# Every second FFN1 chunk of the first block in a bank of attention's pool

## The chip, the cores and the metric

The kernel runs on one core of a Trainium2 chip. The metric is the device time of one execution in microseconds. The core has a matrix engine (PE), a vector engine (DVE), a scalar engine (ACT), a general engine (POOL) and a queue that issues the transfers (SP). Each engine takes its instructions in the order in which they stand in its queue, and waits at the head of the queue until what that instruction needs is there. Matmul results land in eight accumulation banks of 128 x 512 fp32 each.

## The reference

Eight batches of 576 rows go through linear attention with a norm per head, and then through a mixing layer and a two-layer FFN with a residual:

```python
kv = np.einsum('bhsd,bhse->bhde', k, v)
out = np.einsum('bhsd,bhde->bhse', q, kv)
out = out / rms(out) * g_norm                  # rms over the 64 columns of a head
x = out.transpose(0, 2, 1, 3).reshape(B, S, H * D)        # 8 x 576 x 512
u = x + (x.transpose(0, 2, 1) @ U @ V).transpose(0, 2, 1)
y = u + np.maximum(u @ w_ch1, 0.0) @ w_ch2     # 512 -> 2048 -> 512
```

The weights come in as 64-bit floats; the kernel decodes their bits to fp32 itself.

## The kernel before

Attention runs batch by batch and, in a batch, over four pairs of heads. The FFN runs over nine blocks of 512 rows (`j` 0 to 8). A block goes through the 2048 hidden columns in 16 chunks `f` of 128. For a chunk,

- F1(f) (`ffn1`, lines 365 to 367) is 12 matmuls of 128 x 512 into one bank: four slices of the inner dimension, each as three products, because every operand is split into a high and a low part;
- `relu` evicts that bank in two steps: hh(f) on ACT (line 374), the rounded result, and hl(f) on DVE (line 375), what the rounding left over. hl(f) is the last reader of the bank. hh and hl have two buffers each (`hp`);
- F2(f) (`ffn2`, line 382) is 12 matmuls that add to the four output banks `y`: four with hh and the high weights, four with hl, four with hh and the low weights. They run in order of f.

While block 0 runs, the weights of its later chunks are still being decoded: for each 128 x 512 weight tile ACT takes an absolute value (line 80), DVE does four operations (lines 83, 84, 86, 88), ACT rounds the result (line 93), POOL takes the rest (line 94). The loop over the chunks asks for the decode of w1(f+3) and w2(f+3) ahead of chunk f. Beside that the attention of batch 1 is laid into block 0 (`STEPS0`): for each pair p a step kv(p) (lines 194, 198; ACT copies the result with line 101), out(p) (lines 217, 219, and much DVE work up to line 272), t(p) (lines 287, 289; read by lines 301 and 302) and mix(p) (line 357, read by line 359). Each takes one or two banks of the pool `ps_p`, whose tiles are called `pp`. After block 0 the same goes on with batch 2 in block 1, and so on, with no more weights to decode.

The eight banks are four for the outputs `y` (pool `ps_y`), one for FFN1 (`ps_h`, tile `h`), three for attention (`ps_p`, tile `pp`). FFN1 of chunk 0 of block 0 has a `pp` bank already (`hs`, line 485), since it starts ahead of the loop. A new tile of a pool takes a bank that an earlier tile of it has left, and so waits for the last reader of that earlier tile.

The text of the kernel isn't the order on the engines. When the program is built, a scheduler puts the instructions of each engine in an order, by its own estimate of when their operands are there; it also picks which of the three `pp` banks a tile gets. That order is fixed when the kernel runs.

Of the kernel before, what the change touches and what calls it, by code (L numbers as in the profile page):

```python
# [10 lines left out]
F32 = mybir.dt.float32  # L11
# [9 lines left out]
P = 128  # L21
# [8 lines left out]
BLK = 512  # L30
# [17 lines left out]
def build(ctx: ExitStack, tc: tile.TileContext, kv_in, kvt0_in, kvt_in, q_in, uv_in, g_in, w1, w2, out):  # L48
# [10 lines left out]
    ps_h = ctx.enter_context(tc.tile_pool(name="ps_h", bufs=1, space=bass.MemoryType.PSUM))  # L59
    ps_p = ctx.enter_context(tc.tile_pool(name="ps_p", bufs=3, space=bass.MemoryType.PSUM))  # L60
# [91 lines left out]
    def decode_w(which, f, tmp=None, n=None):  # L152
        if tmp is None:
            tmp = st.tile([P, DM], F32, name="st")
        decode(raws.pop((which, f)), tmp, n)
        w = weight_slot(f"{which}s{f}", [P, 2, DM], F32R, which, f)
        if n is None:
            split(w[:, 0], w[:, 1], tmp, nc.gpsimd)
        else:
            move("wh", n, w[:, 0], tmp)  # L160
            minus("wl", n, w[:, 1], tmp, w[:, 0].bitcast(F32))
        w_sb[which][f] = [w[:, s].rearrange("p (d c) -> p d c", c=P) for s in range(2)]
# [199 lines left out]
    def ffn1(h, f, ds, j):  # L362
        uh, ul = ut[j]
        for d in ds:
            nc.tensor.matmul(h, lhsT=w1s[f][0][:, d, :], rhs=uh[:, d, :], start=(d == 0), stop=False)  # L365
            nc.tensor.matmul(h, lhsT=w1s[f][0][:, d, :], rhs=ul[:, d, :], start=False, stop=False)  # L366
            nc.tensor.matmul(h, lhsT=w1s[f][1][:, d, :], rhs=uh[:, d, :], start=False, stop=(d == ND - 1))  # L367

    def relu(h, end=False):
        if end:  # L370
            hh, hl = [sc.tile([P, BLK], F32R, name=f"h{s}_end", tag=f"x{s}") for s in "hl"]
        else:
            hh, hl = [hp.tile([P, BLK], F32R, name=f"h{s}") for s in "hl"]
        nc.scalar.activation(out=hh, in_=h, func=AF.Relu)  # L374
        nc.vector.scalar_tensor_tensor(out=hl, in0=h, scalar=0.0, in1=hh.bitcast(F32), op0=ALU.max, op1=ALU.subtract)  # L375
        return hh, hl

    def ffn2(y, hs):
        for c, cols, acc in y:
            for f, hh, hl in hs:  # L380
                for w, h in ((0, hh), (0, hl), (1, hh)):
                    nc.tensor.matmul(acc, lhsT=w2s[f][w][:, c, :], rhs=h[:, cols], start=(f == 0 and w == 0 and h is hh),  # L382
                                     stop=(f == NF - 1 and w == 1))

    def finish(y, j):
        uh, ul = ut.pop(j)
        for c, cols, acc in y:
            if j == NBLK - 1:
                o = ut32[c][:, S - BLK + cols.start:S - BLK + cols.stop]
                nc.vector.scalar_tensor_tensor(out=o, in0=o, scalar=g_sb, in1=acc, op0=ALU.mult, op1=ALU.add)  # L390
            else:
                o = st.tile([P, DM], F32, name="st")
                nc.vector.tensor_tensor(out=o, in0=acc, in1=uh[:, c, :].bitcast(F32), op=ALU.add)  # L393
                nc.gpsimd.tensor_tensor(out=o, in0=o, in1=ul[:, c, :].bitcast(F32), op=ALU.add)  # L394
            nc.sync.dma_start(out=out[j, c][:, cols], in_=o)

    def outputs(j):

        y = [(c, slice(0, BLK), ps_y.tile([P, BLK], F32, name="y")) for c in range(ND)]
        if j == NBLK - 1:  # L400
            c, _, acc = y.pop()
            y.append((c, slice(0, BLK // 2), acc[:, 0:BLK // 2]))
            y.append((c, slice(BLK // 2, BLK), ps_p.tile([P, BLK], F32, name="pp")[:, 0:BLK // 2]))
        return y
# [85 lines left out]
    def prep_schedule(b):  # L490

        todo = {}
        if 0 < b <= B:
            todo[1] = [lambda: [split_cols(b - 1, c, 1, nc.gpsimd) for c in range(ND)]]
        if b < B:
            for p in range(NPAIR):
                steps = STEPS0 if b == 1 else STEPS
                base = steps["gap"] * p

                def kv(p=p):  # L500
                    kv_step(b, p)
                    nxt = (b, p + 1) if p + 1 < NPAIR else (b + 1, 0)
                    if nxt[0] < B:
                        load_kv(*nxt)

                def o(p=p):
                    for what in (out_step, stats_step, mul_step, xsplit_step, turn_step):
                        what(b, p)
                    nxt = (b, p + 1) if p + 1 < NPAIR else (b + 1, 0)
                    if nxt[0] < B:  # L510
                        load_q(*nxt)

                def t(p=p):
                    t_step(b, p)
                    t4_step(b, p)

                for at, what in (("kv", kv), ("out", o), ("t", t), ("mix", lambda p=p: mix_step(b, p))):
                    todo.setdefault(base + steps[at], []).append(what)
        return todo
# [3 lines left out]
    for j in range(NBLK):  # L523
        todo = prep_schedule(j + 1)
        y = None
        for f in range(NF):
            if j == 0:
                for which in ("w1", "w2"):
                    while ahead[which] < min(NF, f + 1 + AHEAD[which]):
                        decode_w(which, ahead[which])  # L530
                        ahead[which] += 1
            end = False
            if j == 0 and f < NEARLY:
                h = hs[f]
                ffn1(h, f, [3], j)
            else:
                end = j == NBLK - 1 and f == NF - 1
                h = ps_p.tile([P, BLK], F32, name="pp") if end else ps_h.tile([P, BLK], F32, name="h")
                ffn1(h, f, range(ND), j)
            hcur = (f, *relu(h, end))  # L540
            for w in todo.get(2 * f, []):
                w()
            if hprev is not None and not (j == NBLK - 1 and f > NF - 3):
                ffn2(y_prev if f == 0 else y, [hprev])
            if f == 0:
                if j > 0:
                    finish(y_prev, j - 1)
                y = outputs(j)
            for w in todo.get(2 * f + 1, []):
                w()  # L550
            held = (held + [hcur])[-3:]
            hprev = hcur
        y_prev = y
# [59 lines left out]
```

## Time and profile before

| | us |
|---|---|
| median of 3 runs | 943.87 (943.43 to 944.83) |
| the profiled execution | 944.59 |
| its span on the core | 942.8 |
| PE busy in the span | 913.3 (4570 matmul records) |
| DVE busy | 446.0 |
| ACT busy | 255.8 |
| POOL busy | 141.8 |

The profiled execution is 1.8 us longer than its span, for what lies around the first and the last instruction. A matmul record lasts about 0.39 us, but matmuls are pipelined: one starts about 0.23 us after the other when nothing is in the way, and that pitch is what counts. A busy engine of nearly 100% means a queue that never waits; the idle time of an engine is named with what ended it.

In the rows, `h<-uth,w1s` is FFN1, `y<-hh,w2s` and `y<-hl,w2s` are FFN2, `hh<-h` and `hl<-h` the two steps of `relu`, `st<-w1raw,st` and the like the decode of a weight tile. `PE` is the matmul itself, `PEld` the load of its stationary operand.

### The profile page before, as it was taken

The numbers are of one execution on the slowest core, as the hardware profiler recorded it, in microseconds if no ns is written. First come the engines' busy times: TensorE is split into PE (matmuls) and PEld (weight loads), VectorE is DVE, ScalarE is ACT, GpSimd is POOL, SyncE is SP. The second block draws the span as 40 slices with busy tenths as digits, with TensorE's granted clock in tenths as the row PEclk, the third lists the DMA queues.
The fourth block names the chain that finished last, engine by engine and source line by source line (L and its number), as shares of the span: only waits on it lengthen the run. The fifth ranks groups of instructions, "written<-read, shape, count | busy, mean of one in ns | idle before, by whom it ended". The sixth has DMA issues, their size and how long they took to land.

```text
span 942.8 us, 12401 instructions
## 1 busy us (share of the span) xinstructions
PE 913.3 (97%) x4570; PEld 762.8 (81%) x4570; DVE 446.0 (47%) x941; ACT 255.8 (27%) x565; POOL 141.8 (15%) x134
## 2 busy tenths in 40 slices
PE   7879889999999999999999999999999999999998
PEld 7757667888888888888888888888888888888887
DVE  6999997644354435443454344443543331112112
ACT  5534554322222222222232223222322221111110
POOL 4454442200020002000020002000200020002000
PEclk9999999999999999999999999999999999999999
DMA  9951121322121113121222112211211010001001
GB/s 351 407 206 31 36 62 36 122 57 66 42 96 56 54 26 109 44 78 26 74 71 82 27 54 93 73 34 44 91 53 26 13 45 1 1 0 46 1 1 45
DMA packets 45037, 65.50 MB, mean 69 GB/s; under 512 B 9904, under 2 KB 28080, under 8 KB 44976
## 3 DMA queue, kind: packets, MB, share of 16 engines
q1 hardware_dynamic: 44976, 64.71, 20.8%
q8 instruction: 36, 0.59, 0.3%
q14 instruction: 25, 0.20, 0.1%
HBM read 46.97 MB, written 9.44 MB: 60 GB/s over the span
## 4 chain that ended last, share of the span: by engine, by line
PE 85%; DVE 11%; issue 1%; SPq 1%; DMA 1%; ACT 0%; DVEq 0%; ACTq 0%
PE y L382 38%; PE h L365 13%; PE h L366 13%; PE h L367 13%; PE pp L217 2%; PE pp L194 2%; DVE st L86 2%; DVE st L88 1%; DVE st L83 1%; SPq L275 1%; DVE st L84 1%; PE pp L287 1%; PE pp L357 1%; DVE hl L375 1%; PE pp L289 1%
## 5 line engine op out<-in xcount | busy, mean ns | idle before, releaser
L382 PE MATMUL y<-hh,w2s 128*128 128x512 f32 x1144 | 374.7, 395 | 4.6 <-ACT hh L374 3.9
L375 DVE SCALAR_TENSOR_TENSOR hl<-h,hh 128x512 fp32r<-128x512 f32 x142 | 97.6, 688 | 334.2 <-ACT hh L374 334.1
L382 PEld LDWEIGHTS y<-hh,w2s 128*128 128x128 f32 x1144 | 208.4, 189 | 45.8 <-ACT hh L374 5.8
L365 PE MATMUL h<-uth,w1s 128*128 128x512 f32 x568 | 224.6, 395 | 12.6 <-DVE hl L375 12.6
L366 PE MATMUL h<-utl,w1s 128*128 128x512 f32 x568 | 222.9, 393 | 0.0
L382 PE MATMUL y<-hl,w2s 128*128 128x512 f32 (+1 forms) x572 | 222.5, 390 | 0.0
L367 PE MATMUL h<-uth,w1s 128*128 128x512 f32 x568 | 222.3, 391 | 0.0
L374 ACT ACTIVATE hh<-h 128x512 fp32r<-128x512 f32 x142 | 84.8, 597 | 394.4 <-PE h L367 394.2
L365 PEld LDWEIGHTS h<-uth,w1s 128*128 128x128 f32 x568 | 107.3, 189 | 39.3 <-DVE hl L375 14.3
L367 PEld LDWEIGHTS h<-uth,w1s 128*128 128x128 f32 x568 | 107.4, 189 | 23.3
L382 PEld LDWEIGHTS y<-hl,w2s 128*128 128x128 f32 x572 | 108.1, 189 | 21.9
L366 PEld LDWEIGHTS h<-utl,w1s 128*128 128x128 f32 x568 | 107.3, 189 | 21.6
L113 POOL TENSOR_TENSOR xl<-x,xh 128x512 fp32r<-128x512 f32 x32 | 43.2, 1349 | 492.2 <-ACT xh L101 488.3
L394 POOL TENSOR_TENSOR st<-st,utl 128x512 f32<-128x512 f32 x32 | 41.0, 1303 | 154.0 <-DVE st L393 153.7
L359 DVE TENSOR_TENSOR ut<-pp,ut 128x288 f32<-128x288 f32 x56 | 24.7, 456 | 34.0 <-DMA ut<-xt 18.6
L322 ACT ACTIVATE uth<-ut,g_sb 128x448 fp32r<-128x448 f32 (+7 forms) x56 | 27.7, 531 | 43.9 <-DVE ut L359 39.7
L393 DVE TENSOR_TENSOR st<-y,uth 128x512 f32<-128x512 f32 x32 | 21.2, 685 | 34.9 <-PE y L382 25.5
L230 DVE TENSOR_REDUCE ms<-x 128x10 f32<-128x640 f32 x32 | 26.0, 812 | 17.0 <-ACT x L221 17.0
L101 ACT CAST xh<-x 128x640 fp32r<-128x640 f32 x32 | 23.2, 725 | 35.5 <-DVE x L246 35.5
L323 DVE SCALAR_TENSOR_TENSOR utl<-ut,g_sb,uth 128x448 fp32r<-128x448 f32 (+7 forms) x56 | 27.2, 514 | 10.2 <-ACT uth L322 7.3
L194 PE MATMUL pp<-kv_sb 128*128 128x128 f32 x232 | 31.4, 275 | 0.2 <-DVE ts L302 0.2
L194 PEld LDWEIGHTS pp<-kv_sb 128*128 128x128 f32 x232 | 29.3, 191 | 1.6 <-DVE ts L302 0.7
(187 smaller groups left out, 752.0 us busy)
## 6 DMA issues: line engine op xcount, KB each, us to landing
kv_sb<-kv_in SPq DMA_DIRECT2D x29, 512.0 KB, 3.5
q_sb<-q_in SPq DMA_DIRECT2D x29, 288.0 KB, 2.9
w1raw<-w SPq DMA_DIRECT2D x16, 512.0 KB, 9.9
w2raw<-w SPq DMA_DIRECT2D x16, 512.0 KB, 10.2
out<-st SPq DMA_DIRECT2D x32, 256.0 KB, 2.0
ut<-xt SPq DMA_DIRECT2D x224, 20.0 KB, 1.8
ut<-xt SPq DMA_DIRECT2D x224, 16.0 KB, 1.8
kvt_sb<-kvt_in SPq DMA_DIRECT2D x27, 128.0 KB, 3.2
```

Of the source, the lines that this page charges most:

```text
L113: eng.tensor_tensor(out=out, in0=in0, in1=in1, op=ALU.subtract)
L194: nc.tensor.matmul(pp[:, 0:P], lhsT=m[:, i * P:(i + 1) * P], rhs=m[:, MAIN + i * P:MAIN + (i + 1) * P], start=(i == 0 and b < NATIVE), sto ...
L230: nc.vector.tensor_reduce(out=ms.rearrange("p (i h) -> p i h", h=2), in_=xv, axis=AX.X, op=ALU.add)
L322: nc.scalar.mul(out=hi, in_=src, mul=g_sb)
L323: nc.vector.scalar_tensor_tensor(out=lo, in0=src, scalar=g_sb, in1=hi.bitcast(F32), op0=ALU.mult, op1=ALU.subtract)
L365: nc.tensor.matmul(h, lhsT=w1s[f][0][:, d, :], rhs=uh[:, d, :], start=(d == 0), stop=False)
L366: nc.tensor.matmul(h, lhsT=w1s[f][0][:, d, :], rhs=ul[:, d, :], start=False, stop=False)
L367: nc.tensor.matmul(h, lhsT=w1s[f][1][:, d, :], rhs=uh[:, d, :], start=False, stop=(d == ND - 1))
L374: nc.scalar.activation(out=hh, in_=h, func=AF.Relu)
L375: nc.vector.scalar_tensor_tensor(out=hl, in0=h, scalar=0.0, in1=hh.bitcast(F32), op0=ALU.max, op1=ALU.subtract)
L382: nc.tensor.matmul(acc, lhsT=w2s[f][w][:, c, :], rhs=h[:, cols], start=(f == 0 and w == 0 and h is hh), stop=(f == NF - 1 and w == 1))
L394: nc.gpsimd.tensor_tensor(out=o, in0=o, in1=ul[:, c, :].bitcast(F32), op=ALU.add)
```

## The change

In block 0, the odd chunks 1, 3, ..., 15 get their FFN1 bank from the attention pool `ps_p` instead of from `ps_h`. The even chunks keep the one bank of `ps_h`, and chunk 0 and all other blocks are as before. No instruction is added or taken away.

```diff
@@ -535,7 +535,7 @@
                 ffn1(h, f, [3], j)
             else:
                 end = j == NBLK - 1 and f == NF - 1
-                h = ps_p.tile([P, BLK], F32, name="pp") if end else ps_h.tile([P, BLK], F32, name="h")
+                h = ps_p.tile([P, BLK], F32, name="pp") if end or (j == 0 and f % 2) else ps_h.tile([P, BLK], F32, name="h")
                 ffn1(h, f, range(ND), j)
             hcur = (f, *relu(h, end))
             for w in todo.get(2 * f, []):
```

The scheduler makes another order of it, on every engine. In the rows below, `w1s3` is the decoded first weight of chunk 3, `w2raw15` the raw second weight of chunk 15; the number behind a tile's name tells tiles of one pool apart.

PE, block 0, behind F2(2) of the order before. `hh_766` is hh(2), `hh_872` hh(3), `h_934` the bank of F1(4):

```order
L382 MATMUL y_620<-hl_767,w2s2_598 128x512
L382 MATMUL y_617<-hh_766,w2s2_598 128x512
L382 MATMUL y_618<-hh_766,w2s2_598 128x512
L382 MATMUL y_619<-hh_766,w2s2_598 128x512
L382 MATMUL y_620<-hh_766,w2s2_598 128x512
L382 MATMUL y_617<-hh_872,w2s3_607 128x512
L382 MATMUL y_618<-hh_872,w2s3_607 128x512
L382 MATMUL y_619<-hh_872,w2s3_607 128x512
L382 MATMUL y_620<-hh_872,w2s3_607 128x512
L365 MATMUL h_934<-uth_391,w1s4_647 128x512
```

F1(3) stands ahead of these rows, and the first part of F2(3) comes at once behind F2(2). The same place in the order of the change, from the end of F1(4) on; `pp_770` is the bank of kv(1), `pp_794` and `pp_799` those of out(1), `pp_859` the new bank of F1(3), which is the very bank that kv(1) had:

```order
L365 MATMUL h_934<-uth_391,w1s4_647 128x512
L366 MATMUL h_934<-utl_392,w1s4_647 128x512
L367 MATMUL h_934<-uth_391,w1s4_647 128x512
L194 MATMUL pp_770<-kv_sb_639 128x128 x4
L198 MATMUL pp_770<-kvt_sb_182 128x128
L217 MATMUL pp_794<-kvb1_95,q_sb_721 128x128 x4
L219 MATMUL pp_799<-kvb1_95,q_sb_721 128x128
L365 MATMUL pp_859<-uth_391,w1s3_580 128x512
L366 MATMUL pp_859<-utl_392,w1s3_580 128x512
```

F1(4) now runs ahead of F1(3), and F1(3) stands behind kv(1) and out(1) of attention; F2(3) and F2(4) come behind it. In the same manner F1(5) is now behind F1(6), out(2) and t(1), and F1(7) behind F1(8), out(3) and t(2).

ACT, block 0, before: hh(3) (`hh_872`) and hh(4) (`hh_947`) stand among the casts of the weights of chunks 4 and 5.

```order
L374 ACTIVATE hh_872<-h_859 128x512
L93 CAST w1s4_647<-st_641 128x512
L80 ACTIVATE st_744<-w2raw5_192 128x512
L93 CAST w2s4_656<-st_650 128x512
L93 CAST w1s5_741<-st_735 128x512
L80 ACTIVATE st_841<-w1raw6_194 128x512
L374 ACTIVATE hh_947<-h_934 128x512
```

ACT with the change: the copies of kv(1) (`kvb1_95<-pp_770`, two of them) come behind the cast of w2(7).

```order
L93 CAST w2s7_931<-st_925 128x512
L80 ACTIVATE st_1037<-w2raw8_204 128x512
L101 COPY kvb1_95<-pp_770 64x64 x2
L80 ACTIVATE st_1142<-w1raw9_206 128x512
L93 CAST w1s8_1034<-st_1028 128x512
```

They release the bank that F1(3) takes. Some rows further on the same queue, hh(3) and hh(4) come only behind the cast of w1(9).

```order
L93 CAST w2s8_1043<-st_1037 128x512
L93 CAST w1s9_1148<-st_1142 128x512
L80 ACTIVATE st_1207<-w1raw10_210 128x512
L232 ACTIVATE ta_805<-ms_803 128x10
L374 ACTIVATE hh_872<-pp_859 128x512
L374 ACTIVATE hh_947<-h_934 128x512
```

The two evictions stand side by side now, some five weight chunks later than before.

DVE, the end of the decode, before: `hl_1545` is hl(13).

```order
L88 SCALAR_TENSOR_TENSOR st_1493<-w2raw15_232,st_1493 128x512
L233 RECIPROCAL r0_1105<-ta_1106 128x10
L234 TENSOR_TENSOR ta_1106<-r0_1105 128x10
L235 TENSOR_TENSOR ta_1106<-ta_1106,ms_1104 128x10
L236 TENSOR_SCALAR ta_1106<-ta_1106 128x10
L237 TENSOR_TENSOR r0_1105<-r0_1105,ta_1106 128x10
L244 TENSOR_TENSOR x_85<-pp_1095,r0_1105 128x512
L246 TENSOR_TENSOR x_85<-pp_1100,r0_1105 64x128
L375 SCALAR_TENSOR_TENSOR hl_1545<-h_1531,hh_1544 128x512
```

The same place with the change: `hl_1239` is hl(7), `hl_1312` hl(8).

```order
L234 TENSOR_TENSOR ta_1106<-r0_1105 128x10
L88 SCALAR_TENSOR_TENSOR st_1493<-w2raw15_232,st_1493 128x512
L235 TENSOR_TENSOR ta_1106<-ta_1106,ms_1104 128x10
L236 TENSOR_SCALAR ta_1106<-ta_1106 128x10
L237 TENSOR_TENSOR r0_1105<-r0_1105,ta_1106 128x10
L244 TENSOR_TENSOR x_85<-pp_1095,r0_1105 128x512
L246 TENSOR_TENSOR x_85<-pp_1100,r0_1105 64x128
L375 SCALAR_TENSOR_TENSOR hl_1239<-pp_1225,hh_1238 128x512
L375 SCALAR_TENSOR_TENSOR hl_1312<-h_1298,hh_1311 128x512
```

Up to the last decode operation (line 88 of w2(15)) DVE has the same instructions in both orders, but for the evictions hl: 13 of them, hl(0) to hl(12), before, and 7, hl(0) to hl(6), with the change; lines 233 and 234 of the last pair moved ahead of it.

## The prediction

> **What bounds the kernel now.** I read the chain of waits first, to see which engine sets the end, and then the busy times by stretch, cut where PE stops idling.
>
> ```profile
> PE 85%; DVE 11%; issue 1%; SPq 1%; DMA 1%; ACT 0%; DVEq 0%; ACTq 0%
> ```
> ```profile
> core 0: us, PE busy (x) PEld busy (x) DVE busy (x) ACT busy (x) POOL busy (x), PEclk, DMA share, GB/s
> 48.00:149.30 101.30, 83.88 (x375) 65.27 (x376) 99.62 (x164) 47.89 (x93) 44.84 (x31) 0.95 0.23 80
> 149.30:170.00 20.70, 20.62 (x107) 17.02 (x105) 13.64 (x32) 7.57 (x17) 3.56 (x3) 1.00 0.15 47
> 170.00:939.00 769.00, 769.00 (x3818) 645.69 (x3817) 293.36 (x664) 176.12 (x394) 72.00 (x56) 1.00 0.16 49
> ```
>
> There are two regimes. From 48 to 149 us DVE is full (99.62 of 101.30) and PE idles for 17.4 us: block 0 goes at the pace of the weight decode. From 149 us on PE is full to the end. So the end is set thus: whatever matmul work is undone when DVE lets go is added, microsecond for microsecond, and nothing later has slack to give it back. The change touches the first regime alone; the question is how much PE work it leaves behind at its end.
>
> What PE waits for in the first regime, by groups of instructions from 48 to 150 us (busy us, mean ns | idle before, and what ended it):
>
> ```profile
> L365 PE MATMUL h<-uth,w1s 128*128 128x512 f32 x48 | 21.0, 438 | 12.6 <-DVE hl L375 12.6
> L382 PE MATMUL y<-hh,w2s 128*128 128x512 f32 x98 | 32.8, 412 | 4.4 <-ACT hh L374 3.9 <-ACT w2s L93 0.6
> L84 DVE TENSOR_SCALAR st<-st 128x512 uint32<-128x512 uint32 x26 | 16.2, 623 | 0.1
> L375 DVE SCALAR_TENSOR_TENSOR hl<-h,hh 128x512 fp32r<-128x512 f32 x12 | 8.2, 679 | 1.2 <-ACT hh L374 1.2
> ```
>
> 12.6 us of its idle time is FFN1 waiting for hl of the chunk before, which leaves the one bank late since it stands among the decode operations (line 84 and the like) of a queue that hardly ever waits. That is the wait that a second bank would take away, if the bank were free.
>
> **Where the new bank comes from.** By the order with the change F1(3) takes the bank that kv(1) had, so it needs line 101's copy of kv(1), and that copy stands on ACT behind the cast of w2(7). hh(3) stands behind the cast of w1(9). ACT takes its queue in order, so these positions are times. ACT's rows of before give them (`w1s` at 91.62 is w1(8), the one at 98.44 w1(9), the `w2s` row w2(7)):
>
> ```profile
> 88.17 0.70 ACT L80 ACTIVATE st<-w2raw 128x512 f32<-128x512 f32 x1 [1.29 <-POOL w1s L94]
> 89.05 0.62 ACT L93 CAST w2s<-st 128x512 fp32r<-128x512 f32 x1 [0.19 <-DVE st L88]
> 91.62 0.62 ACT L93 CAST w1s<-st 128x512 fp32r<-128x512 f32 x1 [1.95 <-DVE st L88]
> 92.15 0.42 ACT L101 COPY kvb<-pp 64x64 f32<-64x64 f32 x2
> 98.44 0.62 ACT L93 CAST w1s<-st 128x512 fp32r<-128x512 f32 x1 [0.21 <-DVE st L88]
> ```
>
> These casts wait for DVE, whose decode stays the same; only evictions move off from ahead of it. One hl costs 0.60 us of DVE's queue (from its start to that of the next row, below). Ahead of w2(7)'s last decode operation stand 6 of them before and 3 with the change: 89.05 - 1.8 = 87.2 us for the cast, and with 0.62 for it, 0.70 for an absolute value and 0.42 for the copies the bank is free at about 89. Ahead of w1(9)'s stand 7 before and 3 now: 98.44 - 2.4 = 96.0, so hh(3) starts at about 97. F2(3) can't start sooner, and F2(4), F1(6) and the rest stand behind it on PE. In the run of before F2(3) started at 64.09:
>
> ```profile
> 61.32 1.07 PE L382 MATMUL y<-hh,w2s 128*128 128x512 f32 x4
> 64.09 1.20 PE L382 MATMUL y<-hh,w2s 128*128 128x512 f32 x4 [1.70 <-ACT hh L374]
> 67.26 0.76 PE L365 MATMUL h<-uth,w1s 128*128 128x512 f32 x1 [1.97 <-DVE hl L375]
> 67.82 0.63 PE L366 MATMUL h<-utl,w1s 128*128 128x512 f32 x1
> 68.25 0.63 PE L382 MATMUL y<-hl,w2s 128*128 128x512 f32 x1
> ```
>
> So PE does F1(4) and kv(1), and then has nothing for nearly 20 us; FFN work falls some 33 us behind. It doesn't catch up in this regime: F1(5) waits for t(1), whose line 302 stands on DVE between the operations of w1(12), and F1(7) for t(2), behind w1(15)'s third. FFN is tied to the pace of attention's pairs, and these to the decode.
>
> **How much is left when DVE lets go.** hl(7) is the last eviction that stands behind the decode; from there PE is free. The end of the decode on DVE, before:
>
> ```profile
> 149.05 0.68 DVE L88 SCALAR_TENSOR_TENSOR st<-w2raw,st 128x512 uint32<-128x512 uint32 x1
> 150.71 0.69 DVE L244 TENSOR_TENSOR x<-pp,r 128x512 f32<-128x512 f32 x1
> 151.31 0.27 DVE L246 TENSOR_TENSOR x<-pp,r 64x128 f32<-64x128 f32 x1
> 151.51 0.67 DVE L375 SCALAR_TENSOR_TENSOR hl<-h,hh 128x512 fp32r<-128x512 f32 x1
> 152.11 0.83 DVE L272 STREAM_TRANSPOSE xt<-x 128x640 f32<-128x640 f32 x1
> ```
>
> 151.51 is hl(13), 152.11 the next row: 0.60 us for an hl. With the change hl(7) stands where hl(13) stood, behind the same rows less six evictions: 151.5 - 6 x 0.6 = 147.9, done at 148.6. PE then has, by its order: 8 matmuls of F2(7), 12 each of F2(8) to F2(15) and of F1(9) to F1(15), and F1(0) of block 1, which stands ahead of F2(15): 8 + 96 + 84 + 12 = 200. The pitch, and the same point in the run of before:
>
> ```profile
> 148.93 0.39 PE L382 MATMUL y<-hl,w2s 128*128 128x512 f32 x1
> 149.16 0.39 PE L382 MATMUL y<-hh,w2s 128*128 128x512 f32 x1
> 163.29 0.42 PE L357 MATMUL pp<-v,t 128*128 128x288 f32 x2
> 163.55 0.28 PE L192 MATMUL pp<-tails 128*128 128x256 f32 x1
> 164.48 1.18 PE L382 MATMUL y<-hh,w2s 128*128 128x512 f32 x4
> 169.36 0.39 PE L365 MATMUL h<-uth,w1s 128*128 128x512 f32 x1
> ```
>
> The pitch is 0.227 us: in the chain of waits eight FFN2 matmuls in a row take 1.81 us.
>
> ```profile
> 161.64 1.81 PE y L382 x8
> ```
>
> 200 x 0.227 = 45.4 us. Attention between them is t(3), nine small matmuls, and four of line 357. The latter take 0.13 each (163.29 to 163.55 for two); t of a pair takes 0.62:
>
> ```profile
> 95.32 0.30 PE L287 MATMUL pp<-xh,u 128*64 128x128 f32 x1
> 95.94 0.45 PE L382 MATMUL y<-hh,w2s 128*128 128x512 f32 x1
> ```
>
> Together 1.1, so the work ends at 148.6 + 45.4 + 1.1 = 195.1 us. Before, F2(15) was through at 169.36; of F1(0) of block 1 three matmuls were left then (0.7 us), while kv of batch 2, 163.55 to 164.48 or 0.93 us, was done already, which the new order has later. The same work ended at 169.36 + 0.7 - 0.93 = 169.1. **Difference: 26.0 us.**
>
> Two small terms come on top. F2(9) stands close behind F1(9) and has to wait for hh(9); such a wait cost 0.69 us before:
>
> ```profile
> 75.55 1.20 PE L382 MATMUL y<-hh,w2s 128*128 128x512 f32 x4 [0.69 <-ACT hh L374]
> ```
>
> Then the clock. Behind the waits of 1.70 and 1.97 us above, matmuls start 0.43 us apart (67.82 to 68.25), at half pace. With the change PE idles far longer, and F1(3), F1(5) and F1(7) will run at half pace; in the DVE-bound stretch that costs nothing as long as their hh come no later than ACT's queue gets to them. Behind 148.6 it costs until the clock is back: between nothing and 2.4 us, if a whole group of 12 starts 0.43 - 0.227 = 0.20 us late each (an estimate from these rows). I take 0.8, as F1(7) and F2(7) end shortly ahead. Sum: 26.0 + 0.7 + 0.8 = 27.5 us.
>
> The profiled execution took 944.6, so 972.1; the median of the runs shown is 0.7 under it: **971.4 us**. Bounds of its own: down to 24.3 us if DVE's own 1.7 us of idle (101.30 - 99.62) go and the two small terms are nothing (968); up to 32.4 if two groups at half pace, 2.4 us each, hold up the decode (976).
>
> By the Trainium skill (TensorE: Matmul & The Clock Gate, "What's actually happening") PE's clock falls to half after an idle window of about 3.4 us and comes back after as long a busy one; the trace has it fall behind two waits of under 2 us with a little work between, so the window is not one unbroken wait here. By that rule alone the last term would be at most 1.7 us in place of 0.8.
>
> **The rivals.** *The second bank does what it can:* FFN1 of odd chunks starts while hl of the chunk before is pending, and the 12.6 us go. For it: that wait is the largest of PE in the stretch. The point is the time of F1(3): if its bank were free by about 67 us, PE would be ahead; 944.6 - 12.6 = 932.0, as a median 931.3. Against it: the bank is kv(1)'s, whose copy is queued behind the decode of chunk 7. *DVE sets the pace anyway:* all decode is as before, FFN keeps up some other way, and the time stays 943.9. For it DVE's 99.62 of 101.30; against it that its queue holds six evictions fewer ahead of its end, which is the very sign that FFN is behind. The Trainium skill (the same page, "HAM oscillation — how this bites in real kernels") reports a kernel for which double-buffered PSUM gave no further gain (126.6 to 125.5 us); by it this rival would be the result. No run here shows that kernel. *The late evictions block ACT:* behind hh(3), hh(5) and hh(7) on ACT stand casts and absolute values of the decode. If the FFN1 chunk ahead of them is at half pace, 12 x (0.43 - 0.227) = 2.4 us each, and comes after ACT's queue has got there, the decode itself stops; three times that gives 7.3 more, 978.7, and with a late out(1) or t(1) some 985. hh(3) has some 2 us of room: the bank is free at 89, out(1) takes 1.0 (94.29 to 95.32 below), F1(3) at half pace 5.2, so 95.2 against 97.
>
> ```profile
> 94.29 1.05 PE L217 MATMUL pp<-kvb,q_sb 128*128 128x128 f32 x8
> ```
>
> *A part of it:* if evictions come some pairs sooner than reckoned, half of the 120 matmuls (200 less 80 that were left before) is left: 944.6 + 14 = 958.
>
> **How the numbers follow.** The forecast 0.70, blocked ACT 0.12, a part 0.08, no change 0.05, faster 0.05. What this kernel's measurement can tell from no change is about 0.2%, 1.9 us. So slower 0.90, same 0.05, faster 0.05. The forecast's own range is 966 to 977; to hold 8 in 10 it takes in the first of the blocked cases and some of the partial ones: 962 to 981.
>
> **What would show it.** Right: an idle stretch of PE from about 70 to 89 us; F2(3) near 97; the first hh of an odd chunk ended by line 101 or ACT's own queue; DVE still full until about 146; PE full from about 149, with block 0 through near 196, and 45 us of idle PE from 48 to 149 in place of 17.4. Wrong: F2(3) before 80, or idle of PE that is spread in small waits as before. If DVE has idle time between 90 and 146, ACT was blocked and the time is above 976. If the time is right but the idle lies behind 200 us, the sum holds by chance.

## The result, and the profile after

| | before | with the change |
|---|---|---|
| median | 943.65 us (943.08 to 944.83, 4 runs) | 971.26 us (968.14 to 973.66, 4 runs) |
| profiled execution | 944.59 us | 968.14 us |
| its span | 942.8 us | 966.4 us |

The ratio of the times is 1.0289, 95% interval 1.0256 to 1.0322: the kernel is 2.9% slower. The forecast was 971.4 us.

The busy times of the changed kernel by stretch, in the columns that the prediction explained (PE, PEld, DVE, ACT, POOL, granted clock of PE, DMA share, GB/s):

```profile
48.00:149.30 101.30, 66.23 (x272) 50.85 (x271) 99.13 (x171) 47.97 (x95) 47.84 (x33) 0.80 0.24 79
149.30:170.00 20.70, 20.27 (x97) 16.65 (x96) 6.21 (x12) 4.66 (x10) 0.00 (x0) 1.00 0.05 12
170.00:196.00 26.00, 26.00 (x121) 21.69 (x120) 7.60 (x11) 2.80 (x5) 3.83 (x3) 1.00 0.08 27
196.00:963.00 767.00, 766.85 (x3808) 643.40 (x3806) 292.82 (x664) 175.29 (x393) 69.23 (x53) 1.00 0.16 49
```

The two regimes are still there. DVE is as full as before (99.13 of 101.30 us), and from 149 us on PE is full. What differs is how much PE got done while DVE was full: 272 matmul records in place of 375. The 103 that are missing were done later, at 0.227 us each: 23.4 us, and the span grew by 966.4 - 942.8 = 23.6. PE stood idle for 101.30 - 66.23 = 35.1 us of that stretch (17.4 before), and its clock there was 0.80 (0.95 before), so part of the loss is not idle time but matmuls at half pace.

The groups of PE's instructions from 48 to 150 us show where the idle time went (busy us, mean ns | idle before, and what ended it):

```profile
L382 PE MATMUL y<-hh,w2s 128*128 128x512 f32 x68 | 23.6, 427 | 6.9 <-ACT hh L374 5.1 <-ACT w2s L93 1.8
L365 PE MATMUL h<-uth,w1s 128*128 128x512 f32 x16 | 7.6, 476 | 3.8 <-ACT w1s L93 3.8
L365 PE MATMUL pp<-uth,w1s 128*128 128x512 f32 x12 | 7.3, 606 | 7.1 <-DVE ts L302 7.1
L217 PE MATMUL pp<-kvb,q_sb 128*128 128x128 f32 x24 | 4.2, 330 | 14.8 <-ACT kvb L101 14.8
```

The 12.6 us for which FFN1 waited for hl of the chunk before are gone altogether. In their place stand 14.8 us ended by line 101, the copy of kv(1), and 7.1 us ended by line 302, which reads t. Both are operations of attention, and FFN1 of an odd chunk had to do with neither before.

The long wait itself, in PE's rows (start, duration, what; in brackets the idle time before it and what ended it):

```profile
68.97 1.31 PE L194 MATMUL pp<-kv_sb 128*128 128x128 f32 x8
70.21 0.48 PE L198 MATMUL pp<-kvt_sb 64*128 64x128 f32 x2
85.54 2.07 PE L217 MATMUL pp<-kvb,q_sb 128*128 128x128 f32 x8 [14.84 <-ACT kvb L101]
87.69 0.77 PE L365 MATMUL pp<-uth,w1s 128*128 128x512 f32 x1
95.48 1.21 PE L382 MATMUL y<-hh,w2s 128*128 128x512 f32 x4 [3.71 <-ACT hh L374]
```

The row at 87.69 is F1(3), the one at 95.48 F2(3), which ran at 64.09 before. ACT's rows beside them, with w2(7)'s cast first:

```profile
83.99 0.62 ACT L93 CAST w2s<-st 128x512 fp32r<-128x512 f32 x1 [1.52 <-DVE st L88]
...
85.08 0.40 ACT L101 COPY kvb<-pp 64x64 f32<-64x64 f32 x2
...
94.76 0.19 ACT L232 ACTIVATE ta<-ms 128x10 f32<-128x10 f32 x1
94.86 0.57 ACT L374 ACTIVATE hh<-pp 128x512 fp32r<-128x512 f32 x1
95.34 0.57 ACT L374 ACTIVATE hh<-h 128x512 fp32r<-128x512 f32 x1
```

kv(1) was through on PE at 70.7 us, but its copy waited in ACT's queue behind the decode of chunk 7 until 85.08. hh(3) has no wait of its own: it starts when ACT's queue gets to it.

### The profile page after: what moved, and what is told of

The parts are those of the page before. It is cut to its first block, busy times and chain, and to the rows that moved or that the text cites. A ratio compares the mean times of both kernels' runs of the same rounds, so it can differ in the third digit from the quotient of the medians.

```text
span 966.4 us, 12396 instructions
## 1 busy us (share of the span) xinstructions
PE 919.5 (95%) x4570; PEld 767.9 (79%) x4570; DVE 445.1 (46%) x941; ACT 255.2 (26%) x565; POOL 142.4 (15%) x134
## 4 chain that ended last, share of the span: by engine, by line
PE 85%; DVE 8%; DMA 6%; issue 1%; SPq 0%; ACT 0%; DVEq 0%
PE y L382 38%; PE h L365 12%; PE h L366 12%; PE h L367 12%; DMA w1raw<-w 3%; PE pp L217 2%; PE pp L194 2%; DVE st L86 2%; DMA w2raw<-w 2%; DVE st L88 2%; DVE st L83 1%; DVE st L84 1%; DMA q_sb<-q_in 1%; PE pp L287 1%; PE pp L357 1%
## 5 line engine op out<-in xcount | busy, mean ns | idle before, releaser
L375 DVE SCALAR_TENSOR_TENSOR hl<-h,hh 128x512 fp32r<-128x512 f32 x134 | 92.3, 689 | 341.3 <-ACT hh L374 341.3
L365 PE MATMUL h<-uth,w1s 128*128 128x512 f32 x536 | 211.5, 395 | 3.8 <-ACT w1s L93 3.8
L367 PE MATMUL h<-uth,w1s 128*128 128x512 f32 x536 | 210.0, 392 | 0.7 <-POOL w1s L94 0.7
L366 PE MATMUL h<-utl,w1s 128*128 128x512 f32 x536 | 210.0, 392 | 0.0
L374 ACT ACTIVATE hh<-h 128x512 fp32r<-128x512 f32 x134 | 80.0, 597 | 393.7 <-PE h L367 393.7
L365 PEld LDWEIGHTS h<-uth,w1s 128*128 128x128 f32 x536 | 101.2, 189 | 25.8 <-ACT w1s L93 4.3
L367 PEld LDWEIGHTS h<-uth,w1s 128*128 128x128 f32 x536 | 101.1, 189 | 23.2 <-POOL w1s L94 1.4
L366 PEld LDWEIGHTS h<-utl,w1s 128*128 128x128 f32 x536 | 101.3, 189 | 20.3
L217 PE MATMUL pp<-kvb,q_sb 128*128 128x128 f32 x224 | 30.5, 280 | 14.8 <-ACT kvb L101 14.8
L217 PEld LDWEIGHTS pp<-kvb,q_sb 128*128 128x128 f32 x224 | 29.0, 196 | 15.7 <-ACT kvb L101 15.0
```

The costliest lines, as they stand in the source:

```text
L217: nc.tensor.matmul(big[:, i * P:(i + 1) * P], lhsT=qt[:, TAIL + i * P:TAIL + (i + 1) * P], rhs=kb, start=True, stop=True)
```

## The experiments

Each kernel was compared with the kernel before on the same chip. There that kernel took 946.29 us (7 runs) beside the first four experiments and 946.46 (19 runs) beside the last four. All of them compute the whole reference.

The theory under test is that of the prediction: an odd chunk of FFN is tied, through the bank, to the place that a step of attention has on ACT and DVE, which work through the decode; PE falls behind there, and that backlog is run off behind the decode. The main rivals: the loss comes from something else in the new order (the decode becomes longer, evictions block ACT), or a second bank is worth nothing in this kernel anyway.

### One odd chunk alone: chunk 3, and chunk 1

```diff
-  ... if end else ps_h.tile(...)
+  ... if end or (j == 0 and f == 3) else ps_h.tile(...)
```

> The condition is j == 0 and f == 3: chunk 3 alone takes a bank of attention's pool; all other chunks have FFN1's own bank. In its order 10 evictions hl stand ahead of the last decode operation on DVE (13 before the change, 7 with it), and behind hl(10) 128 FFN matmuls of block 0 and F1(0) of block 1 are left. Theory (matmul work that is left when the decode ends): hl(10) at 151.5 - 3 x 0.6 = 149.7 plus about 2 us for attention's rows that DVE has ahead of it; the end of the block 12 to 14 us later than before, so 955 to 958 us. F2(3) at 90 to 97 as with the whole change. Rival, the half clock alone sets the loss: the idle stretch ahead of F1(3) is the same, so a loss of at most 5 us, 948. Rival, the other seven odd chunks do the harm: 944.

Measured: 958.34 us (957.9 to 963.3), ratio 1.0141 (1.0100 to 1.0182). The one chunk has the same long wait as the whole change. PE's rows, out(1) and F2(3), and the busy times of the two halves of the stretch (columns as above):

```profile
86.49 2.08 PE L217 MATMUL pp<-kvb,q_sb 128*128 128x128 f32 x8 [15.64 <-ACT kvb L101]
96.42 2.07 PE L382 MATMUL y<-hh,w2s 128*128 128x512 f32 x4 [4.42 <-ACT hh L374]
...
48.00:100.00 52.00, 25.52 (x99) 19.47 (x100) 51.60 (x79) 22.99 (x43) 25.11 (x17) 0.77 0.30 109
100.00:149.30 49.30, 45.91 (x222) 36.56 (x222) 48.65 (x96) 25.56 (x54) 22.10 (x15) 0.97 0.18 53
```

From 48 to 100 us PE idles for 52.00 - 25.52 = 26.5 us here and for 25.7 with the whole change, 9.2 before. But from 100 to 149.3 us it idles for 3.4 us (9.4 with the whole change, 8.2 before): with no further odd chunk in attention's pool FFN has the work to fill some of that idle time, and makes up a part of its lag. So about half of the loss, 12 us, comes with F1(3) alone, and the rest with the odd chunks behind it, which keep FFN from catching up. The two parts don't simply add, as the chunks from 9 on show below.

The same edit with `f == 1`:

> The condition is j == 0 and f == 1: chunk 1 alone takes a bank of attention's pool. Its place in the program is ahead of kv(1) and out(1), two of the three banks are free then, and 13 evictions stand ahead of the last decode operation, as before the change. Theory (it's the place behind attention's steps in the pool that costs): no difference, 0 to 1 us. Rival (taking a chunk out of FFN1's own bank costs as such, about 27.6 / 8 = 3.5 us a chunk): 3 to 4 us slower.

Measured: 945.08 us (942.52 to 947.46, 10 runs), ratio 0.9995 (0.9977 to 1.0013), no difference. Chunk 1 takes a bank that is free early (no PE row from 34 to 54 us has a wait), so it is not a chunk in attention's pool as such that costs time. Neither does it gain: FFN1 still waits 10.6 us for hl, because the later chunks have the one bank.

```profile
L365 PE MATMUL h<-uth,w1s 128*128 128x512 f32 x48 | 21.1, 439 | 10.6 <-DVE hl L375 10.6
```

### Odd chunks from 9 on

```diff
+  ... if end or (j == 0 and f > 8 and f % 2) else ps_h.tile(...)
```

> The condition is j == 0 and f > 8 and f odd: only chunks 9, 11, 13 and 15 take a bank of attention's pool. 9 evictions hl stand ahead of the last decode operation, 152 FFN matmuls behind hl(9). Theory: hl(9) at 151.5 - 4 x 0.6 = 149.1 plus some 3 us for attention's rows ahead of it; the end of the block 17 to 20 us later, 961 to 964 us. No long idle stretch of PE ahead of 100 us. Rival, what costs is the wait of F1(3) for kv(1) at 70 to 89 us: it is not there, so the time is that of before, 944. Rival, the half clock alone: at most 5 us.

Measured: 971.17 us (968.54 to 975.75), ratio 1.0270 (1.0226 to 1.0314). This is a miss: half as many chunks cost nearly as much as all of them, 24.9 us. It also shows that the wait of F1(3) isn't needed for the loss: from 48 to 100 us PE idles for 8.2 us here, less than before. The waits stand elsewhere. PE's rows with waits, from F1(9)'s surroundings:

```profile
123.07 2.08 PE L194 MATMUL pp<-kv_sb 128*128 128x128 f32 x8 [6.03 <-DVE ts L302]
141.90 0.61 PE L357 MATMUL pp<-v,t 128*128 128x288 f32 x1 [4.74 <-DVE ts L302]
150.58 0.37 PE L287 MATMUL pp<-xh,u 128*64 128x128 f32 x1 [6.09 <-ACT xh L101]
152.62 0.79 PE L365 MATMUL pp<-uth,w1s 128*128 128x512 f32 x1 [1.09 <-DVE ut L359]
153.21 0.63 PE L366 MATMUL pp<-utl,w1s 128*128 128x512 f32 x1
```

F1(9) starts at 152.62, in a bank that a mix step of attention had. By the order it stands on PE behind the steps of three pairs, and PE waits with them: it idles for 25.7 us from 100 to 149.3 us (8.2 before) and for 2.6 more up to 170. The clock is the second half of the miss: F1(9)'s matmuls start 0.43 us apart, and PE was at half clock from 116.9 to 157.9 us in one piece. My expectation had counted the matmuls left over behind the decode (152 behind hl(9)) as if PE were free and at full clock from there. The mechanism is that of the theory, a chunk tied to a late step of attention, but its price was mis-sized: a loss of 17 to 20 us was expected, and 971.17 - 946.29 = 24.9 was measured.

### The second bank without attention's banks

Does the second bank gain anything if it is nobody else's? There are eight banks, so it has to be taken from attention for good. Two kernels separate the two effects: before with two banks for attention, and the same with the third as an own bank of FFN's odd chunks.

```diff
-    ps_p = ... tc.tile_pool(name="ps_p", bufs=3, ...)
+    ps_p = ... tc.tile_pool(name="ps_p", bufs=2, ...)
```

> The kernel before with two banks in attention's pool in place of three, in the whole program; nothing else. Control for the next run: what attention loses by a bank. 13 evictions stand ahead of the last decode operation, as before. Theory: block 0 as before; attention's steps come a little later, and block 1 can wait for its inputs for some us: 944 to 950. Rival (the change loses its time because attention has a bank less): the loss of the change is seen here too, 960 to 971.

```diff
+    ps_o = ... tc.tile_pool(name="ps_o", bufs=1, ...)
+  ... if end else (ps_o.tile(..., name="ho") if j == 0 and f % 2 else ps_h.tile(...))
```

> The odd chunks of block 0 take a bank that nothing else uses, and attention has two banks, as in the run before. 13 evictions stand ahead of the last decode operation; F1(f+1) stands ahead of F2(f) all through block 0. Theory (it's the sharing with attention's pool that costs, not the second bank): no loss against the run with two banks; the 12.6 us that FFN1 waited for hl mostly go, but PE work left at the end of the decode is the same (59 matmuls against 56), so the time is 0 to 5 us under that run: 940 to 948. Rival (a second FFN1 bank as such makes the order worse): 960 or more. Rival (the whole wait of 12.6 us comes off the time): 932 to 936.

Measured: 953.74 us (953.64 to 953.90) for two banks, ratio 1.0081 (1.0048 to 1.0113), and 963.16 us (961.47 to 963.85) with the own bank, ratio 1.0174 (1.0134 to 1.0214). Both lie above what was expected, the second by 15 us and on the wrong side of the first. On this chip the kernel before took 946.29, 2.6 us more than in the first comparison.

The own bank does what a second bank is thought to do. No F1 group waits for hl any more from 48 to 150 us, only for weights; a part of that wait, 7.2 of the 12.6 us, has moved to F2, which needs hl too. Still block 0's last F2 matmul starts at 160.88, where it was at 169.13 before:

```profile
L365 PE MATMUL h<-uth,w1s 128*128 128x512 f32 x27 | 10.9, 403 | 0.5 <-ACT w1s L93 0.5
L365 PE MATMUL ho<-uth,w1s 128*128 128x512 f32 x24 | 9.6, 400 | 0.8 <-ACT w1s L93 0.8
L382 PE MATMUL y<-hl,w2s 128*128 128x512 f32 x55 | 24.0, 436 | 7.2 <-DVE hl L375 7.2
...
160.88 0.39 PE L382 MATMUL y<-hh,w2s 128*128 128x512 f32 x1
162.81 0.24 PE L287 MATMUL pp<-xh,u 128*64 128x128 f32 x1 [1.55 <-DVE x L244]
```

And then PE has nothing to do. Its rows behind that, and the busy times of the next stretches:

```profile
165.80 0.57 PE L357 MATMUL pp<-v,t 128*128 128x288 f32 x1 [2.07 <-DVE ut L359]
172.08 0.79 PE L365 MATMUL h<-uth,w1s 128*128 128x512 f32 x1 [1.40 <-ACT uth L322]
179.29 0.61 PE L365 MATMUL h<-uth,w1s 128*128 128x512 f32 x1 [1.08 <-ACT uth L322]
...
149.30:170.00 20.70, 16.33 (x83) 12.93 (x82) 12.57 (x29) 6.24 (x16) 5.09 (x4) 0.90 0.22 68
170.00:200.00 30.00, 25.89 (x111) 20.40 (x110) 13.37 (x35) 8.71 (x22) 2.66 (x2) 0.78 0.33 104
```

Block 1's FFN1 waits for `uth`, the input that attention of batch 1 makes. The 8 us that FFN was ahead are lost, since attention came later. Its step out(3) starts on PE at 133.72 us in the kernel before, at 147.74 with two banks and at 154.50 with the own bank, and the fourth and last 128 x 448 piece of `uth` is rounded on ACT (line 322) at 165.97, 169.66 and 178.58. So of its 12.6 us of lateness 3.7 came with the two banks and 8.9 with the own bank, in whose order more of FFN stands ahead of attention: block 0's last F2 matmul starts 6.4 us behind out(3), and 35.4 us behind it in the kernel before. The granted clock was low as well (0.78 from 170 to 200 us, 1.00 before); what the lateness and the clock each cost in time is not separated. These runs do show that the rival "the second bank does what it can" (12.6 us gained) isn't reached by a bank that FFN has to itself, when attention pays for it: hl is late for F2 as well, and block 0 also has to deliver the next block's input.

### Attention one chunk later, without and with the change

If the position of kv(1) is the cause, the loss must move when that position moves. `STEPS0` tells at which half chunk the steps of a pair are written, so two more is one chunk.

```diff
-STEPS0 = dict(kv=1, out=2, t=6, mix=11, gap=3)
+STEPS0 = dict(kv=3, out=4, t=8, mix=13, gap=3)
```

> The kernel before, with all steps of batch 1's attention asked for one chunk later in block 0 (STEPS0 with kv 3, out 4, t 8, mix 13 in place of 1, 2, 6, 11). Control for the next run. 13 evictions ahead of the last decode operation, 56 matmuls behind hl(13) as before. Expected: within 2 us of the kernel before, or some us slower if block 1 then waits for its inputs.

> The changed kernel with the same shift. In the program F1(3) now comes ahead of kv(1) and out(1), F1(5) behind kv(2) and out(2)'s predecessors. Theory (the place in the pool's queue sets it): F2(3) near 62 to 66 us in place of 95.5; the first long idle stretch of PE moves to F1(5), whose bank is kv(1)'s or later; 11 evictions ahead of the last decode operation and 107 matmuls behind hl(11), so the block ends at 175 to 179 us against 168 without the change: 8 to 14 us slower than the control, about half of the loss of the change. Rival (a second bank for odd chunks harms wherever attention stands): the full loss of 24 to 28 us against the control.

Measured: without the change 946.91 us (943.36 to 949.59, 10 runs), ratio 1.0006 (0.9984 to 1.0029), so the shift by itself is free. With the change 958.82 us (957.00 to 960.58), ratio 1.0158 (1.0130 to 1.0186): 11.9 us over its control, where the change without it costs 22.8 on the same chip. PE's rows:

```profile
61.71 1.20 PE L382 MATMUL y<-hh,w2s 128*128 128x512 f32 x4 [1.72 <-ACT hh L374]
...
91.35 2.08 PE L194 MATMUL pp<-kv_sb 128*128 128x128 f32 x8 [5.83 <-DVE ts L302]
94.67 0.80 PE L365 MATMUL pp<-uth,w1s 128*128 128x512 f32 x1 [0.52 <-ACT kvb L101]
```

F2(3) is back at 61.71, since F1(3) no longer meets kv(1). The tie is now at F1(5), which starts at 94.67, behind a kv step that waited for t and behind its copy. The change is the same in both kernels, and about half of its price (22.8 us on this chip, from the run below) went with a shift that costs nothing alone. That is the test that I rest the cause on. The other half stayed; the rows tie it to F1(5), and no run moved that. Block 0 came later than expected, too: its last F2 matmul starts at 181.38 (168.18 in the control), where 175 to 179 was expected for the end.

### The change once more

> The changed kernel once more, for how far its own executions differ (968.1 to 973.7 in the first four, with a mean granted clock of 0.979 to 0.974), and on the same chip as the other runs. Theory: the span differs with how long PE's clock is at half around the end of the decode (142 to 160 us); in a profile with a span over 968 us the rows of PE between 143 and 160 us show more matmuls 0.43 us apart, and hl(7) comes at the same time within 1 us. Rival: the decode itself takes longer in those executions, and hl(7) comes some us later.

Measured: 969.26 us (968.48 to 972.02), ratio 1.0269 (1.0246 to 1.0293). The profiled execution had a span of 966.8 us, so no execution of over 968 us was seen from inside, and where the slower ones have their half clock, and whether their decode is longer, stays open. hl(7) starts at 143.98 here (144.03 in the first profile), so its early start isn't an accident of one execution; in both, the decode ends 7 us sooner than before, so the loss doesn't come from a longer decode. The two profiles differ in the clock: from 138 to 145 us it was granted at 0.58 here and at 0.77 in the first, and all twelve matmuls of F1(7) ran at half pace here, for a span 0.4 us longer.

## Why the prediction was right, and where by luck

**The wait (right).** The predicted step: the bank of F1(3) is free at about 89 us, hh(3) starts at about 97 and F2(3) with it, and PE idles from about 70 to 89. Measured: copies at 85.08, hh(3) at 94.86, F2(3) at 95.48, idle from 70.7 to 85.5. All of it is 1.5 to 4 us early, in line with the next step.

**hl(7) (the term that was off).** It was put at 151.5 - 6 x 0.6 = 147.9. DVE's rows at the end of the decode:

```profile
140.85 1.25 DVE L234 TENSOR_TENSOR ta<-r 128x10 f32<-128x10 f32 x1
142.02 0.68 DVE L88 SCALAR_TENSOR_TENSOR st<-w2raw,st 128x512 uint32<-128x512 uint32 x1
...
144.03 0.67 DVE L375 SCALAR_TENSOR_TENSOR hl<-pp,hh 128x512 fp32r<-128x512 f32 x1
```

144.03, so 3.9 us early. A part of this is idle time of DVE: before, it waited 1.2 us for hh ahead of hl (the row of line 375 in the prediction), and with the change not at all, in the same stretch from 48 to 150 us:

```profile
L375 DVE SCALAR_TENSOR_TENSOR hl<-h,hh 128x512 fp32r<-128x512 f32 x4 | 2.7, 677 | 0.0
L375 DVE SCALAR_TENSOR_TENSOR hl<-pp,hh 128x512 fp32r<-128x512 f32 x3 | 2.0, 659 | 0.0
```

My sum had six evictions go but not the wait; it stood only in the lower bound, as DVE's 1.7 us of idle. The other 2.7 us are in the durations of DVE's other operations, which I had kept as they were (see the last section).

**The work left over (right).** From the end of hl(7) at 144.7, 200 matmuls and 1.1 us of attention reach to 144.7 + 45.4 + 1.1 = 191.2. The wait for hh(9) was 0.43 us, put at 0.69:

```profile
156.69 1.20 PE L382 MATMUL y<-hh,w2s 128*128 128x512 f32 x4 [0.43 <-ACT hh L374]
```

That gives 191.6, and the matmul behind the last one of block 0 started at 192.18:

```profile
192.18 0.28 PE L192 MATMUL pp<-tails 128*128 128x256 f32 x1
```

The remaining 0.6 us fits the term for the clock (0.8), but wasn't measured apart.

**The size.** In the profiled execution the loss is 23.6 us, the 27.5 of the sum less the 3.9 by which hl(7) came early: 968.1 us. The median came to 971.26 because most executions of the change are slower than the profiled one. Their span and mean granted clock, with the clock's loss worked out as (1 - clock) x span, which counts half clock as lost also where PE had nothing to do:

| execution of the change | span, us | clock | loss, us |
|---|---|---|---|
| profiled | 966.4 | 0.979 | 20.3 |
| second | 968.4 | 0.977 | 22.3 |
| third | 970.6 | 0.974 | 25.2 |
| fourth | 971.9 | 0.974 | 25.3 |

The spans rise by 2.0, 4.2 and 5.5 us over the first, the losses by 2.0, 4.9 and 5.0. So the half-clocked time differs from execution to execution and the time goes with it, within about a microsecond here. In the run of the change once more it does so less well (966.8 us at 0.977, where the second execution here has 968.4), and that the clock is the cause was not tested. I had allowed 0.8 us for the clock and no spread. The forecast met the median to 0.1 us because two errors came out even: hl(7) came 3.9 us early, and the median lies 3.1 us above the profiled execution, where I had put it 0.7 below, together 3.8. The mechanism and the range were sound; the closeness is chance.

**45 us of idle PE (wrong).** Measured were 35.1. I had turned the whole backlog into idle time, while a good part of it was matmuls at half pace (clock 0.80). The sum didn't use this figure.

**Blocked ACT (a trace of it).** F1(7), seven of its twelve matmuls at half pace, ended behind the point where ACT had got to its eviction, and ACT was held once:

```profile
142.55 0.60 ACT L374 ACTIVATE hh<-pp 128x512 fp32r<-128x512 f32 x1 [2.03 <-PE pp L367]
```

It stood behind the last cast but one of the decode, and DVE had only 101.30 - 99.13 = 2.2 us of idle time in the whole stretch (1.7 before). So the rival was there with 2 us of ACT's time and next to nothing of the path's.

**The other rivals.** *DVE sets the pace anyway* falls with PE's backlog: DVE was done sooner and the kernel slower. The Trainium skill (TensorE: Matmul & The Clock Gate, "HAM oscillation — how this bites in real kernels") has a kernel that gained nothing from double-buffered PSUM; the two kernels here with a second bank for all odd chunks don't agree with that, since the bank in attention's pool cost 28 us and an own one, with a bank less for attention, 17. *The second bank does what it can* falls in the case as given, and the own bank shows that it falls as well when FFN doesn't have to wait for the bank but attention has one less. A second bank that takes none from attention wasn't run, as all eight are in use. *A part of it* falls too: all 200 matmuls were left behind hl(7), and 45.4 us for them fit the end of the block.

## What to carry to other kernels

A second buffer from a pool that another pipeline uses isn't a spare one: its first use is bound to wherever the other pipeline's last reader stands in its engine's queue, and everything behind it on the in-order engine is bound with it. Before counting a wait as gained, read from the order who releases the new buffer and at what time that engine gets there; if that is later than the wait that goes, the change is a loss. And ask what the next stage waits for: FFN that was through 8 us sooner gained nothing here, because its next input was not.

## What was not expected of the hardware

**The clock falls behind short waits, and differs between executions of one program.** In the profile of from 9 on the clock fell at 116.9 us, behind waits of 0.33 and 1.29 us and just ahead of the first long one. It then stayed at half for 41 us at a stretch (granted 0.50 from 116.9 to 157.9), through the waits of 6.03, 4.74 and 6.09 us shown there and the work between them: the 5.3 us of F1(9) at the end ran at half pace. The kernel before has executions that differ, too: among its 19 the fastest span was 941.2 us at a clock of 0.995, and the slowest 947.2 at 0.987. The losses as above, 4.7 and 12.3, are 7.6 apart for 6.0 us of time.

The Trainium skill (TensorE: Matmul & The Clock Gate, "A second HAM failure mode: psum-queue depth-cycling") tells of small idle times between groups of matmuls that make the clock go to and fro. The falls behind waits of under 2 us agree with it, here and in the kernel before (1.70 and 1.97 us); the one stretch of 41 us doesn't go to and fro. No run here shows what sets it off in one execution and not in another.

**A small DVE operation can last until POOL's ends.** A 128 x 10 operation of line 236 took 0.16 us in some places and over 1.1 in others. The rows of the kernel before around one of the long ones, on DVE and on POOL:

```profile
109.41 0.67 DVE L86 SCALAR_TENSOR_TENSOR st<-w1raw,st 128x512 uint32<-128x512 uint32 x1
110.01 1.26 DVE L236 TENSOR_SCALAR ta<-ta 128x10 f32<-128x10 f32 x1
111.19 0.42 DVE L83 TENSOR_SCALAR st<-st 128x512 f32<-128x512 f32 x1
```
```profile
109.61 1.63 POOL L94 TENSOR_TENSOR w2s<-st,w2s 128x512 fp32r<-128x512 f32 x1 [1.69 <-ACT w2s L93]
```

POOL's operation ends at 111.24, and line 236's at 111.27. The Trainium skill (SBUF — State Buffer, "SBUF: two separate sides") says that DVE and GpSimd share a pair of ports as a lock that one of them holds for a whole instruction; these rows agree. So DVE's work in a stretch depends on what meets POOL. The groups of the stretch from 48 to 150 us, before and then with the change:

```profile
L83 DVE TENSOR_SCALAR st<-st 128x512 f32<-128x512 f32 x26 | 13.7, 528 | 0.0
L86 DVE SCALAR_TENSOR_TENSOR st<-w1raw,st 128x512 uint32<-128x512 uint32 x12 | 11.9, 990 | 0.0
L236 DVE TENSOR_SCALAR ta<-ta 128x10 f32<-128x10 f32 x3 | 3.5, 1162 | 0.0
```
```profile
L83 DVE TENSOR_SCALAR st<-st 128x512 f32<-128x512 f32 x26 | 17.1, 656 | 0.0
L86 DVE SCALAR_TENSOR_TENSOR st<-w1raw,st 128x512 uint32<-128x512 uint32 x12 | 10.2, 853 | 0.1
L236 DVE TENSOR_SCALAR ta<-ta 128x10 f32<-128x10 f32 x4 | 0.6, 162 | 0.0
```

The same operations got dearer in one line and cheaper in others when the order changed. That the 2.7 us which hl(7) gained beyond its six evictions and DVE's idle time come from this is read from the durations; no run tested it by itself.
